# Key and query scalings split by token slot in five blocks, with a new issue order

## The chip, the core and the metric

The kernel runs on one core of one Trainium2 chip. Its five engines work from queues of their own, each in order: TensorE (PE) for matrix products, VectorE (DVE), ScalarE (ACT) and GpSimd (POOL) for elementwise work, SyncE (SP) for starting transfers. ACT can start transfers too. The metric is the device time of one execution in microseconds (us). Three runs of the kernel before took 165.88, 166.98 and 167.26 us; the median is 166.98 us.

## What is computed

Two layers follow each other. The first is a gated linear attention, a recurrence over 768 tokens for each of 4 batches and 8 heads of 48 channels; the second is a mixer that first mixes tokens and then channels.

```
for t in range(S):                       # q, k, v, alpha: (4, 8, 768, 48)
    state = alpha[:, :, t, :, None] * state + k_t (outer) v_t
    y[:, :, t] = q_t @ state
x = y as (4, 768, 384)
h  = relu(x^T @ w_tok1) @ w_tok2         # over tokens, 768 -> 256 -> 768
u  = x + h^T
h2 = relu(u @ w_ch1) @ w_ch2             # over channels, 384 -> 1536 -> 384
out = u + h2
```

Inputs and output are float32.

## The kernel before, in words

The recurrence is worked out in blocks. A block is 256 tokens of one batch with all its heads, so there are 12 blocks, numbered n = 0 to 11, three to a batch. A partition holds a pair of neighbouring tokens; the two places in the pair are called slot 0 and slot 1, so an input tile is 128 partitions x 8 heads x 2 slots x 48 channels. Within a block the decay is made from logarithms: `ln` takes the logarithm of alpha, `cum` (on PE, with a triangular matrix) sums it up along the tokens, and `E` and `IE` are the exponentials of the sums and of their negatives. Queries are multiplied by E and keys by IE; then an ordinary masked product of the two gives the part of the attention that lies inside the block, and a state carried from half block to half block gives the rest.

The names of a block's operations, with the block's number behind them:

- `ld_at`, `ld_kt`, `ld_qt`, `ld_vt`: loads of alpha, k, q and v (384 KB each, L534)
- `ln`, `cumw`, `E`, `Et`, `IE` for blocks 0 to 2, where each slot has sums of its own (WIDE); for blocks 3 to 11 `P` (product of the two alphas of a pair, L578), `ln1`, `lnP`, `r1`, `cum`, `E`, `IE`, with one sum per pair. There slot 0 of the keys is first multiplied by alpha of slot 1 (`k0a`, L634), and slot 0 of the queries by an inverse (`q0r`, L638)
- `kk` and `qq` (L642): the scalings of all 768 columns (2 slots x 8 heads x 48) of keys by IE and of queries by E, to bf16. They run on DVE or POOL
- `trk`, `trq` (L655): transposes of scaled keys and queries on PE; `evk`, `evq`: their eviction from PSUM. Blocks 6 to 11 have DMA transposes in their place (`dk`, `dq`) and `pq`
- `G0_`, `G1_` and `mask0_`, `mask1_`: the inner products and their masking (L709, DVE); `vb`, `vs0_`, `vs1_`: v cast to bf16, and its halves exchanged; `ka`, `kb`, `kc`: halves of the scaled keys moved between partitions for the state's product `K`; `s`, `sa`, `sm`: the state; `ia`, `ib`, `y0_`, `y1_`: products into the output; `x0_`, `x1_`: its eviction to a tile x of 128 tokens

The six x of a batch feed its mixer: `t1` (L791), `ht` (relu), `t2` (L796), `u` (sum with x), `up` and `ut` (transposes on PE and their eviction, for batches 0 and 1; DMA transposes `ux` for 2 and 3), `c1` (L815), `rt` (relu, L786 on ACT, L788 on DVE), `c2` (L820), `o` (L824) and `st` (store, L574). A `c1` or `c2` group is three matmuls of 384 columns. The weights come in 16 loads (`ldw_`) and are cast to bf16 by DVE, ACT or POOL (`cw_`).

Nothing decides the order of the work at run time. The table ORDER lists every operation with its engine (t PE, s ACT, v DVE, g POOL, y SP), and each engine gets its operations in the order of that list; the table BUFS gives each tile its buffer. Both were written out by a planner, which worked with the costs that stand in the code beside each operation. `f1_` and `f3_` are one or three fillers: products of zeros on PE whose result nobody uses. Operations marked `port=True` on DVE and POOL are made to follow each other where the list goes from one of the two engines to the other: `shared` (L673) adds a wait for the last such operation of the other engine. Dependences between tiles, and the reuse of a buffer, become semaphore waits. In the kernel before, SP starts all 48 input loads, all weight loads and 22 of the 25 stores, and ACT the other three.

Of the kernel before, what the change touches and what calls it, by code (L numbers as in the profile page):

```python
# [11 lines left out]
ALU = mybir.AluOpType  # L12
# [82 lines left out]
B, H, S, D = 4, 8, 768, 48  # L95
HD, DT, DCH = 384, 256, 1536
NB = 3
NX = 6
KFN = 3
# [16 lines left out]
def build(g):  # L116
# [12 lines left out]
    def attention(n):  # L129
# [5 lines left out]
        def O(name, eng, i, **kw):  # L135
            return P.op(f"{name}{n}", eng, pr(i), **kw)
# [20 lines left out]
        else:  # L157
# [16 lines left out]
        kk = O("kk", either(dve(768), pool_tt(768)), 5, writes=[pkk], reads=[kt, IE], port=True, preds=k_in + [e2],  # L174
               emit=lambda e: g.scaled(e, pkk, kt, IE, wide))
        qq = O("qq", either(dve(768), pool_tt(768)), 5, writes=[pkq], reads=[qt, E], port=True, preds=q_in + [e1],
               emit=lambda e: g.scaled(e, pkq, qt, E, wide))
# [3 lines left out]
        if n < NX:  # L181
            bk, bq = V("one"), V("one")
            trk = O("trk", pe([128] * 8), 8, writes=[bk], reads=[pkk], preds=[kk] + fill("trk", bk),
# [3 lines left out]
            trq = O("trq", pe([128] * 8), 8, writes=[bq], reads=[pkq], preds=[qq] + fill("trq", bq),  # L187
# [3 lines left out]
        else:  # L191
            evk = O("dk", {"SP": (1240.0, 1240.0)}, 9, writes=[tpk], reads=[pkk], preds=[kk],
                    emit=lambda e: g.xbar(tpk, pkk), dma=("x", 1400.0, 1180.0, 480.0))
            tqx = V("tpk")
            xq = O("dq", {"SP": (1240.0, 1240.0)}, 9, writes=[tqx], reads=[pkq], preds=[qq],
# [19 lines left out]
        if turned:  # L215
            vs = [vsw(hf, [vc]) for hf in range(2)]
            kx, kp_in = None, [kk, vc, vs[0]]
            if nst == 2:
                kx = V("kt")
                ka = shift("ka", 9, [kx], [pkk], [kk], lambda e: g.kturn(e, kx, pkk, 0))  # L220
                kb = shift("kb", 9, [kx], [pkk], [kk], lambda e: g.kturn(e, kx, pkk, 1))
                kp_in += [ka, kb, vs[1]]
            kc = shift("kc", 9, [pkk], [], [kk, trk if n < NX else evk] + ([ka] if nst == 2 else []),
# [4 lines left out]
        else:  # L228
            KO = O("K", {"PE": (344.0 if nst == 2 else 172.0, 420.0)}, 9.5, writes=[kp], reads=[pkk, vb],
                   preds=[kk, vc] + fill("K", kp) + ([prev_s[1]] if prev_s and k > 0 and n > NB else []),  # L230
# [146 lines left out]
ut_0_0v G0_3t G1_3t mask1_3v cw_wc11s ldw_wc22y up_0_2t ib3t ka4g q0r4g qq4g c1_0_0_0t c1_0_2_0t ld_at6y y1_3t
c1_0_1_0t ut_0_2s rt_0_0_0v x1_3v mask0_3v rt_0_1_0s ldw_wc24y ldw_wc23y sm1_3g trk4t cw_wc12s c1_0_2_1t c1_0_3_1t
c1_0_0_1t c1_0_1_1t c1_0_4_1t rt_0_2_0v rt_0_3_1s rt_0_1_1v trq4t cw_wc13s rt_0_0_1s rt_0_2_1s cw_wc14g cw_wc15g
rt_0_4_1v c1_0_6_0t c1_0_7_1t ldw_wc25y evq4v c1_0_9_1t y0_3t rt_0_9_1v P5v evk4s rt_0_6_0s x0_3v c1_0_8_1t c1_0_7_0t  # L380
rt_0_7_1s kc4s c1_0_10_1t c1_0_11_1t vb4g kb4g lnP5s rt_0_7_0s k0a5g ln15s ld_vt5y rt_0_10_1v cum5t G1_4t mask1_4v
rt_0_11_1s r15s rt_0_8_1s G0_4t c1_0_4_0t c1_0_3_0t IE5s mask0_4v vs0_4g ld_at7y kk5v c1_0_10_0t c1_0_5_0t c1_0_5_1t
rt_0_4_0s cw_wc20s c1_0_8_0t q0r5v c1_0_9_0t c1_0_6_1t rt_0_3_0s E5s rt_0_8_0s rt_0_5_1s c1_0_11_0t rt_0_5_0s
rt_0_6_1s trk5t qq5v vs1_4v ia4t y0_4t cw_wc21g rt_0_11_0s K4t trq5t evk5v sa0_4v c2_0_1_0t rt_0_9_0s sm0_4v
rt_0_10_0v cw_wc24g sa1_4v P6v ld_at8y sm1_4v kc5v vb5g cw_wc22s c2_0_5_0t c2_0_2_0t evq5s x0_4s cw_wc23s cw_wc25s
lnP6s ld_kt6y c2_0_2_1t c2_0_5_1t t1_1_1_0t G1_5t G0_5t P7g vs1_5g t1_1_1_1t c2_0_1_1t c2_0_1_2t c2_0_5_2t ld_qt6y
c2_0_1_3t c2_0_5_3t vs0_5s mask0_5v ld_at9y ld_vt6y c2_0_2_2t mask1_5v cum6t o_0_1v o_0_5v K5t c2_0_2_3t ia5t y0_5t
ib4t sa0_5v ln16s sm0_5v o_0_2v lnP7s k0a6g y1_4t cum7t t1_1_1_2t t1_1_0_0t x1_4v ib5t E6s y1_5t t1_1_0_1t t1_1_0_2t
x0_5s c2_0_3_0t r16s ln18s t1_1_0_3t x1_5v t1_1_0_4t t1_1_1_3t t1_1_0_5t IE6s t1_1_1_4t q0r6v kk6v t1_1_1_5t c2_0_0_0t
st_0_5y ld_kt7y ht_1_0s ht_1_1s ld_qt7y st_0_1y c2_0_3_1t t2_1_5t vb6s t2_1_0t E7s u_1_5v t2_1_2t t2_1_3t t2_1_4t  # L390
t2_1_1t u_1_2v u_1_3v c2_0_0_1t c2_0_3_2t qq6g ln17s k0a7g c2_0_0_2t u_1_0v c2_0_4_0t up_1_1t u_1_4v c2_0_3_3t u_1_1v
up_1_0t IE7s P8g ut_1_1v dk6y up_1_2t ka6g kb6s ut_1_0s r17s vs0_6s c2_0_4_1t c2_0_0_3t ld_at10y ld_vt7y o_0_3v
ut_1_2v dq6y kk7g dk7y c1_1_10_1t c1_1_9_1t c1_1_1_1t rt_1_10_1v r18s rt_1_1_1s vs1_6g kc6g lnP8s c1_1_2_0t ld_qt8y
P10v o_0_0v K6t vb7s q0r7g c2_0_4_2t cum8t s0_6v sa1_6v P9g c1_1_2_1t c1_1_0_1t c1_1_10_0t c1_1_3_0t qq7g vs1_7g kb7s
ld_vt8y E8s lnP10s rt_1_0_1s rt_1_2_1v rt_1_10_0v ld_kt8y c1_1_4_1t ld_qt9y rt_1_2_0v rt_1_9_1v ka7s vs0_7s sm1_6v
c2_0_4_3t c1_1_7_0t ld_kt9y dq7y c1_1_11_0t ld_vt9y st_0_0y lnP9s IE8s c1_1_8_1t rt_1_4_1s o_0_4v kc7s rt_1_7_0s
c1_1_9_0t cum9t c1_1_11_1t c1_1_1_0t c1_1_0_0t rt_1_8_1s rt_1_11_1s rt_1_1_0s pq6s ln19s q0r8v rt_1_3_0v rt_1_11_0v
rt_1_9_0v c1_1_5_0t qq8g K7t c1_1_5_1t k0a8g rt_1_0_0v rt_1_5_0v c1_1_3_1t rt_1_3_1s rt_1_5_1s c1_1_6_1t c1_1_7_1t
sa0_7v c1_1_4_0t sm0_7v r19s rt_1_7_1s ld_kt10y dq8y sa1_7v c1_1_6_0t rt_1_6_1v IE9s G0_6t G1_6t rt_1_6_0s rt_1_4_0s
kk8g E9s vb8s ln110s vs1_8s pq7s q0r9g ld_qt10y mask0_6v c2_1_4_0t k0a9g c2_1_4_1t dk8y c2_1_1_0t mask1_6v kk9g ib6t  # L400
# [478 lines left out]
```

## Time and profile before

| what | value |
|---|---|
| median of three runs | 166.98 us |
| profiled run, its own time | 167.16 us |
| span of the profiled run | 165.5 us |
| PE busy | 153.9 us, 93% |
| DVE busy | 113.5 us, 69% |
| ACT busy | 98.7 us, 60% |
| POOL busy | 77.4 us, 47% |
| read from HBM | 25.17 MB |
| granted PE clock | 1.0 in every slice |

The span runs from the first to the last instruction of one profiled execution; the run's time has a little around it. Busy times are sums over an engine's instructions. In the views below, an instruction's row gives its start, its duration, its engine and line, the tiles written and read, and in brackets how long the engine stood idle before it and what ended that. Rows that group instructions give their count, the busy time, the mean duration in ns and the idle time before them. The chain that ended last goes back from the last instruction to what released each step.

### The profile page before, as it was taken

How to read it: one execution, taken by the hardware profiler on the slowest of the kernel's cores; microseconds unless marked ns; L12 is line 12 of the kernel's file. 1: busy time of each engine (PE TensorE's matmuls, PEld its weight loads, DVE VectorE, ACT ScalarE, POOL GpSimd, SP SyncE). 2: the span in 40 equal slices, each digit the busy share in tenths (PEclk: the TensorE clock that was granted, in tenths of full speed). 3: DMA queues.
4: the chain of work that ended last, by engine and by line, in shares of the span. 5: the costliest groups of instructions: out<-in, count | busy, mean ns of one | idle time of the engine just before them, and what ended most of it. 6: DMA issues, size and time to landing. Idle time of an engine off the chain costs nothing.

```text
span 165.5 us, 4049 instructions
## 1 busy us (share of the span) xinstructions
PE 153.9 (93%) x1599; PEld 97.9 (59%) x1599; DVE 113.5 (69%) x200; ACT 98.7 (60%) x186; POOL 77.4 (47%) x87
## 2 busy tenths in 40 slices
PE   7849799799999999999999999999899999999992
PEld 2425657376667576665666676665566656566660
DVE  4059999698989987667776888985686703544232
ACT  3776699897999765589899965526502304162100
POOL 4055575899643344876689698397320000000000
PEclk9999999999999999999999999999999999999999
DMA  4999999999999799999999999889401362030114
GB/s 126 318 280 307 275 307 347 350 330 303 263 354 366 199 279 284 270 230 280 218 281 168 263 240 155 189 176 238 120 0 51 111 127 95 19 128 0 48 55 182
DMA packets 76322, 34.46 MB, mean 208 GB/s; under 512 B 68112, under 2 KB 76304, under 8 KB 76304
## 3 DMA queue, kind: packets, MB, share of 16 engines
q1 hardware_dynamic: 75872, 33.63, 78.9%
q10 hardware_dynamic: 432, 0.59, 1.0%
q8 instruction: 12, 0.20, 0.5%
q14 instruction: 6, 0.05, 0.1%
HBM read 25.17 MB, written 4.72 MB: 181 GB/s over the span
## 4 chain that ended last, share of the span: by engine, by line
PE 64%; DMA 13%; POOL 6%; SPq 4%; ACT 4%; issue 3%; DVE 2%; POOLq 0%; DVEq 0%
PE ps L820 26%; PE ps L815 20%; PE ps L593 9%; DMA in<-in_v_dram 6%; DMA in<-in_q_dram 5%; PE ps L791 4%; POOL pkq L642 3%; PE ps L796 3%; SPq L534 3%; DMA tpk<-pkq 3%; PE ps L655 1%; POOL in L638 1%; DVE pkk L642 1%; ACT vb L686 1%; PE ps L807 1%
## 5 line engine op out<-in xcount | busy, mean ns | idle before, releaser
L820 PE MATMUL ps<-wc,rt 128*128 128x384 bf16 (+2 forms) x300 | 53.2, 320 | 0.0
L815 PE MATMUL ps<-ut,wc 128*128 128x384 bf16 x288 | 50.9, 326 | 0.1
L786 ACT ACTIVATE rt<-ps 128x384 bf16<-128x384 f32 x59 | 26.9, 493 | 28.0 <-PE ps L815 27.7
L815 PEld LDWEIGHTS <-wc 128*128 128x128 bf16 x288 | 27.4, 98 | 17.7 <-issue 0.4
L820 PEld LDWEIGHTS <-rt 128*128 128x128 bf16 x300 | 27.6, 98 | 16.7
L709 DVE TENSOR_TENSOR gtm<-ps,mk 128x1024 bf16<-128x1024 f32 x24 | 28.5, 1219 | 4.6 <-PE ps L593 3.4
L788 DVE TENSOR_SCALAR rt<-ps 128x384 bf16<-128x384 f32 x37 | 19.4, 553 | 13.3 <-PE ps L815 13.2
L824 DVE TENSOR_TENSOR o<-ps,u 128x384 f32<-128x384 f32 (+2 forms) x25 | 13.1, 536 | 12.9 <-PE ps L820 12.9
L642 POOL TENSOR_TENSOR pkq<-in,E 128x768 bf16<-128x768 f32 x9 | 16.3, 1816 | 5.2 <-DVE in L638 3.3
L642 POOL TENSOR_TENSOR pkk<-in,IE 128x768 bf16<-128x768 f32 x7 | 12.7, 1817 | 9.4 <-ACT E L626 7.5
L686 ACT CAST vb<-in 64x384 bf16<-64x384 f32 (+1 forms) x22 | 14.1, 640 | 3.6 <-DMA in<-in_v_dram 2.3
L800 DVE TENSOR_TENSOR u<-ps,x 128x384 bf16<-128x384 f32 x24 | 12.1, 552 | 3.9 <-PE ps L796 3.6
L593 PE MATMUL ps<-zs 128*128 128x512 bf16 x30 | 9.7, 457 | 2.6 <-ACT IE L626 1.2
L791 PE MATMUL ps<-x,wt 128*128 128x384 bf16 x48 | 11.1, 326 | 0.0
L796 PE MATMUL ps<-ht,wt 128*128 128x384 bf16 x48 | 9.9, 327 | 0.8 <-POOL wt L687 0.8
L634 POOL TENSOR_TENSOR in<-in,in 128x384 f32<-128x384 f32 x8 | 8.0, 999 | 5.7 <-DVE pkk L687 2.6
L686 ACT CAST x<-ps 128x384 bf16<-128x384 f32 x12 | 5.5, 480 | 7.9 <-PE ps L593 7.8
L754 DVE TENSOR_TENSOR tmp<-ps,ss 128x384 f32<-128x384 f32 x16 | 8.8, 553 | 0.7 <-PE ps L593 0.3
L687 POOL CAST vb<-in 64x384 bf16<-64x384 f32 (+1 forms) x12 | 7.0, 581 | 4.8 <-DMA in<-in_v_dram 2.4
L593 PE MATMUL ps<-tpq,tpk 48*64 48x128 bf16 (+1 forms) x288 | 8.2, 219 | 0.8 <-POOL tpq L687 0.7
L757 POOL TENSOR_TENSOR ss<-tmp,E 128x384 bf16<-128x384 f32 x9 | 7.5, 834 | 3.0 <-PE ps L593 1.6
L593 PE MATMUL ps<-vb,gtm 128*128 128x48 bf16 x192 | 8.7, 184 | 0.0
(91 smaller groups left out, 208.2 us busy)
## 6 DMA issues: line engine op xcount, KB each, us to landing
in<-in_alpha_dram SPq DMA_DIRECT2D x12, 384.0 KB, 5.4
in<-in_q_dram SPq DMA_DIRECT2D x12, 384.0 KB, 5.6
in<-in_k_dram SPq DMA_DIRECT2D x12, 384.0 KB, 5.6
in<-in_v_dram SPq DMA_DIRECT2D x12, 384.0 KB, 5.5
in<-in_moe_w_ch_dram SPq DMA_DIRECT2D x12, 384.0 KB, 6.3
out_dram<-o SPq DMA_DIRECT2D x20, 192.0 KB, 2.4
in<-in_moe_w_tok_dram SPq DMA_DIRECT2D x4, 384.0 KB, 5.5
out_dram<-o ACTq DMA_DIRECT2D x3, 192.0 KB, 1.9
```

What stands on the lines that cost most here:

```text
L593: return self.pe.matmul(out, lhsT=lhsT, rhs=rhs, start=start, stop=stop, skip_group_check=True)
L642: self.shared(self.eng[e].tensor_tensor(self.t(dst)[:, :, :, 0:D], self.t(src).rearrange("p h s d -> p s h d"), bass.AP(tensor=f.tensor, o ...
L686: return self.act.copy(d, s)
L709: self.nc.vector.tensor_tensor(self.t(gtm)[:, hf, :, :], self.pair(gp).rearrange("p a (j t) -> p (a j) t", t=128), bass.AP(tensor=m.tensor ...
L786: self.act.activation(d, s, AF.Relu)
L788: self.nc.vector.tensor_scalar_max(d, s, 0.0)
L791: self.pe.matmul(self.bank(bank)[:, 0:HD], lhsT=self.wt1[:, kc, m * 128 : m * 128 + 128], rhs=self.t(x), start=(kc == 0), stop=(kc == NS - 1))
L796: self.pe.matmul(self.bank(bank)[:, 0:HD], lhsT=self.wt2[:, kc, i * 128 : i * 128 + 128], rhs=self.t(hts[kc]), start=(kc == 0), stop=(kc = ...
L800: self.nc.vector.tensor_tensor(self.t(u)[:, i % 3], self.bank(bank)[:, 0:HD], self.t(x), ALU.add)
L815: self.pe.matmul(self.bank(bank)[:, 0:HD], lhsT=self.wc1[:, kc, mc * 128 : mc * 128 + 128], rhs=self.t(ut)[:, 3 * half : 3 * half + 3, kc, ...
L820: self.pe.matmul(self.bank(bank)[:, 0 : cz - ca], lhsT=self.t(rts[mc][0])[:, i * 128 : i * 128 + 128], rhs=self.wc2[:, mc, ca:cz], start=( ...
L824: self.nc.vector.tensor_tensor(self.t(o)[:, ca:cz], self.bank(bank)[:, 0 : cz - ca], self.t(u)[:, i % 3, ca:cz], ALU.add)
```

## The change

Blocks 0 to 4 (SPLIT) scale keys and queries in two instructions of 384 columns each, one per slot. `kk` and `qq` are then the half of slot 1, which in blocks 3 and 4 depends on the load only; `kl` and `ql` are the half of slot 0, which waits for `k0a` or `q0r`. Whoever read the whole result now waits for both halves. The tables ORDER and BUFS are new throughout.

```
+SPLIT = (0, 1, 2, 3, 4)
...
-        kk = O("kk", either(dve(768), pool_tt(768)), 5, writes=[pkk], reads=[kt, IE], port=True, preds=k_in + [e2],
-               emit=lambda e: g.scaled(e, pkk, kt, IE, wide))
-        qq = O("qq", either(dve(768), pool_tt(768)), 5, writes=[pkq], reads=[qt, E], port=True, preds=q_in + [e1],
-               emit=lambda e: g.scaled(e, pkq, qt, E, wide))
+        slots = ((1,), (0,)) if n in SPLIT else ((0, 1),)
+
+        def scale(names, dst, src, f, pre, raw):
+            return [O(nm, either(dve(384 * len(sl)), pool_tt(384 * len(sl))), 5, writes=[dst], reads=[src, f], port=True,
+                      preds=(pre if 0 in sl else raw) + ([e2] if f is IE else [e1]),
+                      emit=lambda e, sl=sl: g.scaled(e, dst, src, f, wide, sl)) for nm, sl in zip(names, slots)]
+
+        kk = scale(("kk", "kl"), pkk, kt, IE, k_in, [ld["kt"]])
+        qq = scale(("qq", "ql"), pkq, qt, E, q_in, [ld["qt"]])
...
-    def scaled(self, e, dst, src, f, wide):
-        f = self.t(f)
+    def scaled(self, e, dst, src, f, wide, slots):
+        f, c, z = self.t(f), slots[0], len(slots)
         self.shared(self.eng[e].tensor_tensor(
-            self.t(dst)[:, :, :, 0:D], self.t(src).rearrange("p h s d -> p s h d"),
-            bass.AP(tensor=f.tensor, offset=f.offset, ap=[list(f.ap[0]), [HD if wide else 0, 2], [D, H], [1, D]]),
-            ALU.mult))
+            self.t(dst)[:, c : c + z, :, 0:D], self.t(src)[:, :, c : c + z, :].rearrange("p h s d -> p s h d"),
+            bass.AP(tensor=f.tensor, offset=f.offset + (c * HD if wide else 0),
+                    ap=[list(f.ap[0]), [HD if wide else 0, z], [D, H], [1, D]]), ALU.mult))
```

What the new tables change, in the parts that the prediction speaks of:

| | before | after |
|---|---|---|
| fillers (single products of zeros) | 30 | 33, of which 7 (before 13) ahead of the first sums |
| input loads issued by SP / ACT | 48 / 0 | 29 / 19 |
| stores issued by SP / ACT | 22 / 3 | 13 / 12 |
| weight casts on ACT / POOL / DVE | 10 / 6 / 0 | 7 / 8 / 1 |
| `ht` on ACT / DVE | 5 / 3 | 7 / 1 |
| first loads in order | at0 at1 at3 qt0 kt0 vt0 vt1 kt1 at2 | at0 kt0 at1 vt0 qt0, at3 (ACT), kt1 at2 |

ACT's list up to the two relus of the first token product, after the change (`ld_` are the loads that it issues):

```
ln0 ln1 E0 ld_at3 IE0 IE1 Et1 vb0 E1 Et0 ld_qt2 evq0 ln13 ln2 vb1 ld_kt3 lnP3 vs0_0 IE2 Et2 E2 ld_vt2 IE3 vs1_1 E3 evq1
x1_0 evq2 x0_0 vb2 vs0_1 cw_wt10 r13 x0_1 vs1_2 lnP4 kb3 vb3 ka3 x0_2 vs1_3 ld_qt4 kc3 ht_0_1 ht_0_0
```

and before:

```
ln0 ln1 E0 Et0 ln13 IE0 IE1 E1 vb0 r13 vb1 vs0_0 lnP3 Et1 ln2 Et2 E2 IE2 evq1 x0_0 x1_0 E3 IE3 lnP4 vb2 evq2 cw_wt10
cw_wt11 x0_1 x1_1 vs1_2 vb3 vs1_3 vs0_3 kc3 ht_0_1
```

POOL's list from block 3 on, after: `q0r3 ql3 cw_wc10 cw_wc11 k0a4 kk4 kl4 q0r4 qq4 ql4 cw_wc14`; before: `q0r3 cw_wt20 qq3 k0a4 cw_wc10 kk4 ka4 q0r4 qq4`. The halves stand on DVE for block 0 (all four), block 2 (all four) and qq3, and on POOL for block 1, kk3, kl3, ql3 and block 4. The last piece of the output, in columns 0 to 319 and 320 to 383, was finished with the wide part last and is now finished with the narrow part last.

150 lines of the change are left out of this document (75 added, 75 removed), and 22 rows, old and new, of the table BUFS.

## The prediction

> **What bounds the kernel now.** I read the page's first part, then the busy time by stage, then the chain that ended last, and then each engine's instructions in order of time up to the first channel matmul.
>
> ```profile
> span 165.5 us, 4049 instructions
> ...
> PE 153.9 (93%) x1599; PEld 97.9 (59%) x1599; DVE 113.5 (69%) x200; ACT 98.7 (60%) x186; POOL 77.4 (47%) x87
> ```
>
> The span is 165.5 us of a run that took 167.16 us, so 1.66 us lie outside it. TensorE is busy for 153.9 us of it.
>
> ```profile
> 25.00:30.00 5.00, 4.87 (x87) 3.54 (x83) 5.00 (x7) 4.59 (x9) 2.57 (x5) 1.00 1.12 347
> 30.00:35.00 5.00, 3.71 (x37) 2.31 (x38) 3.50 (x8) 4.19 (x8) 5.00 (x5) 1.00 1.11 339
> ...
> 110.00:120.00 10.00, 9.42 (x61) 5.64 (x60) 6.33 (x14) 5.70 (x13) 6.32 (x8) 1.00 0.73 172
> ```
>
> ```profile
> 36.50:70.00 33.50, 33.50 (x342) 22.44 (x339) 28.70 (x46) 25.89 (x52) 18.97 (x22) 1.00 1.02 292
> ```
>
> ```profile
> 70.00:94.70 24.70, 24.26 (x262) 15.20 (x260) 18.40 (x33) 23.13 (x44) 18.67 (x16) 1.00 1.17 243
> ```
>
> In these rows the first pair after the length is PE, the third DVE, the fourth ACT, the fifth POOL. From 36.5 to 70 us PE never stops; between 70 and 94.7 us it loses 24.70 - 24.26 = 0.44 us, and between 110 and 120 us 0.58 us. So after 36.5 us about 1.0 us (these two) is all that a better order could win back on PE. Before that PE idles or runs fillers, and the time is set by how soon the first channel matmul, c1_0_0_0, can start.
>
> ```profile
> 31.64 1.62 PE L796 MATMUL ps<-ht,wt 128*128 128x384 bf16 x8 [0.85 <-POOL wt L687]
> ...
> 33.42 0.62 PE L655 MATMUL ps<-idn,pkq 128*128 128x128 bf16 x8 [0.16 <-POOL pkq L642]
> ...
> 36.52 1.14 PE L815 MATMUL ps<-ut,wc 128*128 128x384 bf16 x6
> ...
> 41.07 0.61 PE L655 MATMUL ps<-idn,pkq 128*128 128x128 bf16 x8
> ```
>
> ```profile
> 21.99 7.64 DMA in<-in_q_dram
> ...
> 29.77 0.99 POOL in L638
> 30.76 0.82 POOL wt L687
> ...
> 162.22 0.49 DVE o L824
> ```
>
> The first fence is PE's own order, the second the chain that ended last. c1_0_0_0 starts at 36.52 us. The second token product (L796) waited 0.85 us for a weight cast on POOL, which stood behind q0r3, which waited for the load of qt3; trq3 at 33.42 us waited 0.16 us for the query scaling on POOL. I count the PE work ahead of c1_0_0_0 in both orders: it is the same set of operations, fillers aside. Hence the sum: time after = time before + shift of c1_0_0_0 + change of PE's waits behind it + change of the tail behind PE's end at 162.22 us.
>
> **The change, part by part.** *The two halves.* The rows of the groups by shape:
>
> ```profile
> L642 POOL TENSOR_TENSOR pkq<-in,E 128x768 bf16<-128x768 f32 x9 | 16.3, 1816 | 5.2 <-DVE in L638 3.3 <-DVE pkk L642 1.7
> ...
> L638 POOL TENSOR_TENSOR in<-in,lf 128x384 f32<-128x384 f32 x5 | 5.0, 996 | 2.2 <-DMA in<-in_q_dram 1.4 <-ACT la L584 0.7
> ...
> L642 DVE TENSOR_TENSOR pkk<-in,IE 128x768 bf16<-128x768 f32 x5 | 4.8, 953 | 0.0
> ...
> L638 DVE TENSOR_TENSOR in<-in,lf 128x384 f32<-128x384 f32 x4 | 2.2, 554 | 0.0
> ```
>
> A scaling of 384 columns is not in the trace; the nearest rows are L638's products of that size. Two of them are 2 x 996 - 1816 = 176 ns dearer on POOL and 2 x 554 - 953 = 155 ns on DVE. Of the ten scalings of blocks 0 to 4, five have both halves on POOL (kk1, qq1, kk3, kk4, qq4), four on DVE (block 0 and block 2), and that of block 3's queries is shared. That adds 0.9 us to POOL and 0.6 us to DVE, at least nothing and at most this, since queued instructions overlap a little. What it can win is an early start of the raw half, and the order uses it little: in blocks 0 to 2 neither half needs another product first, and in block 4 both halves are queued behind k0a4 and q0r4 or next to them. Only qq3 (DVE) goes ahead of its other half, by which trq3 comes free of the 0.16 us wait. DVE's extra is hidden by ACT, as the next part shows; without that cover it is 0.6 us. POOL's pair in block 4 is not hidden, see below.
>
> *Loads on ACT's queue.* This is the larger part: 19 of the 48 input loads and 12 stores are now issued by ACT, where before 3 stores were. What an issue costs:
>
> ```profile
> 0.81 0.46 SPq L534
> ...
> 1.33 0.56 SPq L534
> ...
> 1.94 1.26 SPq L534
> ```
>
> ```profile
> L534 SPq DMA_DIRECT2D in<-in_q_dram x12: 433/1150/1507, 3.2 to 106.2; - x12
> ```
>
> ```profile
> L574 ACTq DMA_DIRECT2D out_dram<-o x3: 338/377/444, 156.6 to 161.0; - x3
> ```
>
> SP's first two loads took 0.46 and 0.56 us, all others while the queue was full 1.15 us in the median; ACT's three stores, late and alone, 0.377 us. ACT has one load under way at a time, so I take 0.45 us, near the first row, and keep 0.38 and 1.15 us as the ends. The Trainium skill, page "DMA: Bandwidth & Descriptors", section "Issuing engines are not separate DMA queues", says that transfers started from several engines run on the same DMA engines and interleave, and that only the issuing sequencer's time is saved. The trace agrees as far as it goes: the DMA share in the rows above is already 1.12 and 1.11 at 25 to 35 us with one queue. By that rule nothing is gained in transfer time; without it the 19 loads could shorten the stream, so it lowers the chance of my faster case.
>
> ```profile
> 4.44 0.84 ACT L587 ACTIVATE la<-in 128x768 bf16<-128x768 f32 x1 [2.35 <-DMA in<-in_alpha_dram]
> 5.62 0.84 ACT L587 ACTIVATE la<-in 128x768 bf16<-128x768 f32 x1 [0.34 <-DMA in<-in_alpha_dram]
> ...
> 31.88 0.83 ACT L686 CAST wt<-in 128x768 bf16<-128x768 f32 x1 [0.56 <-DMA in<-in_moe_w_tok_dram]
> ```
>
> ```profile
> 8.95 0.96 DVE L642 TENSOR_TENSOR pkq<-in,E 128x768 bf16<-128x768 f32 x1 [5.61 <-DMA in<-in_q_dram]
> ```
>
> These are landings seen by those who waited: the first load 4.44 us, the second 5.62, the fourth 8.95, the 21st (wt2's second piece) 31.88: (31.88 - 4.44) / 20 = 1.37 us a load. The loads ahead of that piece are the same 20 in both orders, so it still lands near 31.9 us. One wait is new: SP's issue of wt1's second piece takes the buffer of qt1 and so waits for qq1 on POOL, near 19 us (10.3 us for qt0 as worked out below, four halves on DVE, seven shorter products and copies on POOL); vt3, qt3 and both pieces of wt2 stand behind it on SP. By then 15 loads are issued, and at 1.37 us each they last to 4.44 + 14 x 1.37 = 23.6 us, which covers the stop. But at1 is now third: 5.62 + (8.95 - 5.62) / 2 = 7.3 us, so ACT's ln1 starts 1.6 us later.
>
> *ACT up to the relus of the token hidden (ht).* Pitches, start to start:
>
> ```profile
> 22.24 0.52 ACT L584 ACTIVATE la<-in 128x384 bf16<-128x384 f32 x1
> 22.67 0.81 ACT L686 CAST vb<-in 128x768 bf16<-128x768 f32 x1
> 23.39 1.31 ACT L686 COPY tpq<-ps 128x1024 bf16<-128x1024 bf16 x1
> 24.61 0.83 ACT L686 CAST wt<-in 128x768 bf16<-128x768 f32 x1
> ...
> 30.25 0.49 ACT L786 ACTIVATE ht<-ps 128x384 bf16<-128x384 f32 x1
> ```
>
> 384 columns take 0.43 us, 768 take 0.72, 1024 take 1.22. Before, ACT issues from ln1 to ht_0_1 14 of 768, 2 of 1024, 16 of 384 and 3 tiny ones (0.1): 10.1 + 2.4 + 6.9 + 0.3 = 19.7 us, from 5.62 us; ht's start at 30.25 us shows about 5 us of waits in it. After, from ln1 to the second ht: 13 of 768, 3 of 1024 (evq0 comes from DVE), 20 of 384 (both ht, vs1_1, vs0_1, ka3, kb3 and x0_2 come, vs0_3 and x1_1 go), 3 tiny, and 5 loads: 9.4 + 3.7 + 8.6 + 0.3 + 2.25 = 24.2 us. From 7.3 us that ends at 31.5 us without any wait. Going down the queue I find about 0.9 us that stay: vb2 behind vt2's load, which ACT itself issues only after E2, and little else, as more queued work swallows waits. So both ht are done at 32.4 us (ends: 31.5, and 34 with half of before's waits), and the token product starts there instead of at 31.64 us.
>
> DVE's x copies come before that. In the row
>
> ```profile
> 28.05 1.08 DVE L687 CAST x<-ps 128x384 bf16<-128x384 f32 x2
> ```
>
> the last two x of batch 0 ended at 29.1 us. qt0 is now the fifth load, 8.95 + 1.37 = 10.3 us, so DVE starts 1.4 us later; evq0 (1.2), kk1 and kk3 (0.95 each) leave it, block 0's key halves and k0a3 (0.55 each) and three splittings (0.16 each) come, a net of -1.0 us. So DVE ends its x near 29.5 us, and ACT its own last one, x0_2, five entries ahead of the end, at 32.4 - 4 x 0.43 - 0.45 = 30.2 us: 0.7 us of cover for DVE. Behind ht, ACT casts wt2's second piece, makes E4, IE4 and ln14, evicts trq3 and then copies ut_0_1: 32.4 + 0.72 + 0.43 x 3 + 1.22 + 0.43 (r14) + 0.72 = 36.8 us, where c1_0_0_0 starts: **+0.2 us** (36.52 before). The wait on POOL goes, since the wt2 cast is now DVE's, and ACT is late in its place. Ends: -1.3 us (wt2's piece at 31.9 + cast 0.7 + product 0.3 + sum 0.5 + transposes 0.5 + copy 0.7, and some issue gaps, makes 35.2 us) and +3.3 us (1.15 us an issue).
>
> *trq4.* On POOL now stand cw_wc10, cw_wc11, k0a4, kk4, kl4, q0r4, qq4, ql4. kt4's load went behind both weights and is the 24th: 4.44 + 23 x 1.37 = 35.9 us. Six products of 996 ns end at 42.0 us. PE reaches trq4 after ten channel groups of three matmuls (0.49 us each) and two small y: 36.8 + 4.9 + 0.4 = 42.1 us; before, it was there at 41.07 us. A tie; with the qt4 load of ACT pushing in between I take **+0.3 us** (0 to 1). Nothing else waits there but PE's order behind it.
>
> *Second mixer's channel stage.* From the first c1_1 to the first t1_2 ACT had 39 x 0.43 + 3 x 0.72 + 3 x 1.22 = 22.6 us to do beside PE's 24.7 us (the row 70.00:94.70 covers almost all of it). After, it has 43, 2 and 3 and six loads: 18.5 + 1.4 + 3.7 + 2.7 = 26.3 us, beside PE's stage that grew by four c2 groups to about 26.6 us. An engine that full, in order, with waits, will hold PE's banks now and then: before lost 0.44 us at 92%, I take 1.2 us at 99%: **+0.8 us** (0 to 4).
>
> *Tail.*
>
> ```profile
> out_dram<-o SPq DMA_DIRECT2D x1, 160.0 KB, 1.8
> ...
> out_dram<-o SPq DMA_DIRECT2D x1, 32.0 KB, 1.5
> ```
>
> The last eviction was of 320 columns (0.49 us) and its store 1.8 us; now the 64-column piece is last, and the large one overlaps twelve narrow matmuls: **-0.4 us** (0 to -0.5).
>
> Sum: 0.2 + 0.3 + 0.8 - 0.4 = +0.9 us, so 168.1 us against 167.16 us of the profiled run; the median of 166.98 us is 0.18 us lower, so I predict **167.9 us**. About 1% (1.7 us) is what measuring this kernel can tell from no change.
>
> **The rivals.** *ACT late in both places* (0.20): waits persist as before, ht ends at 34 us, +1.5 us at c1_0_0_0, and the c1_1 stage gives 26.3 us plus half of 2 us of waits, +1.8 us; trq4 is then free; -0.4: 170 us. For it: ACT's busy 23.13 of 24.70 us. Against: waits shrink as queues fill.
>
> *An ACT issue costs 1.15 us* (0.10): +3.3 us at c1_0_0_0, 6 x 0.7 = 4.2 us more in the c1_1 stage, most of it on PE: about 174 us. It decides from some 0.6 us an issue. Against: the rows of ACT's stores.
>
> *Faster* (0.20): ACT's queue has the slack that I deny it, c1_0_0_0 starts 1.3 us earlier, SP, freed of loads, ends half of the 1.0 us of waits, and the tail gives 0.4: -2.2 us, 164.8 us. For it: both waits of the token product on POOL are gone. Against: 24.2 us of queue from 7.3 us on.
>
> *A cold PE* (0.06):
>
> ```profile
> 4.02 0.15 PEld L593 LDWEIGHTS <-zs 128*128 128x128 bf16 x1 [0.28 <-issue]
> 4.45 0.15 PEld L593 LDWEIGHTS <-zs 128*128 128x128 bf16 x1 [0.28 <-issue]
> ```
>
> ```profile
> 8.88 1.02 PE L593 MATMUL ps<-zs 128*128 128x512 bf16 x4 [1.21 <-ACT IE L626]
> ```
>
> The first fillers follow each other by 0.43 us, later ones by about 0.25. Only 7 instead of 13 now stand ahead of the first sums, and then nothing until ln0 ends at 5.3 us. If PE stays at the slow pace until 16 us, trq0, K0, trk0 and trk1 (0.6 us each) double, DVE ends 2.4 us later and, past its cover and ACT's three entries ahead of ht, c1_0_0_0 0.9 us: 168.8 us. The Trainium skill, page "TensorE: Matmul & The Clock Gate", section "What's actually happening", puts the faster clock after about 3.4 us of sustained activity; by that rule this happens, and 7 x 0.43 = 3.0 us of fillers are a little short of it.
>
> That the halves do nothing is no rival in time: I already give them almost none.
>
> **How the numbers follow.** My case has 0.44, with its own range 166.7 to 169.2 us. Faster by over 1% (below 165.3) is nearly all of the faster case, 0.18; slower by over 1% (above 168.65) is ACT's two cases, half of the cold one and the upper end of mine, 0.40; the rest 0.42. The range 164.8 to 170.5 leaves out the dear issue and the edges.
>
> **What would show it.** ACT's two ht end near 32.4 us and c1_0_0_0 starts near 36.8 us; ACT issues of 0.4 to 0.5 us; trq4 near 42.1 us with a wait for POOL of under 1 us; halves of about 1.0 and 0.55 us; PE's waits behind 36 us near 2.1 us, most where c1_1 runs, named after ACT. PE waits of several us after 100 us, which I did not work out, or a load stream off its 1.37 us would make it wrong.

## The result, and the profile after

The changed kernel takes 167.90 us in the median (166.40 to 169.47) where the kernel before, measured beside it, takes 166.64 us: a ratio of 1.0072, with a 95% interval of 1.0044 to 1.0100. It is a little slower, by less than the 1% named above. Ratios and intervals leave out executions more than 1.5% above the fastest of the same kernel and medians keep them, which matters below for e5 alone: its four longest, 169.10 to 170.36 us, are not in its ratio. The profiled execution of the changed kernel took 168.94 us, one of its longer ones, at a mean PE clock of 0.98; its start of the channel stage is therefore set further down beside that of e6, the changed kernel with 14 fillers more, at clock 1.00.

The first parts of the page of the changed kernel:

```profile
span 167.2 us, 4054 instructions
## 1 busy us (share of the span) xinstructions
PE 156.6 (94%) x1602; PEld 99.8 (60%) x1602; DVE 112.6 (67%) x203; ACT 99.3 (59%) x191; POOL 74.4 (45%) x89
...
PEclk9969998799999999999999999999999999999999
```

The span is 1.7 us longer, and PE's clock, full in every slice before, is 6 to 8 tenths in three slices of the first fifth. PE's own order, with the rows that answer to those quoted of before:

```profile
25.82 0.50 PE L599 MATMUL ps<-vb,pkk 64*128 64x96 bf16 x8 [1.75 <-ACT vb L692]
...
37.93 4.06 PE L821 MATMUL ps<-ut,wc 128*128 128x384 bf16 x24
...
43.21 0.61 PE L661 MATMUL ps<-idn,pkq 128*128 128x128 bf16 x8
```

The state product of block 2, K2, waits 1.75 us for ACT's cast of v. The first channel matmul, c1_0_0_0, starts at 37.93 us, 1.41 us later than before (36.52); the transposes trq4 wait for nothing. The stretches behind it:

```profile
5.00:10.00 5.00, 3.36 (x29) 1.78 (x29) 0.74 (x2) 3.07 (x5) 0.00 (x0) 0.76 1.17 324
10.00:15.00 5.00, 4.57 (x64) 3.14 (x63) 3.36 (x7) 4.49 (x9) 3.49 (x5) 0.90 1.17 325
15.00:20.00 5.00, 5.00 (x68) 3.10 (x66) 4.50 (x8) 4.56 (x10) 2.71 (x3) 1.00 1.15 335
20.00:25.00 5.00, 3.93 (x52) 2.49 (x52) 4.71 (x7) 2.92 (x5) 3.02 (x4) 1.00 1.15 337
25.00:30.00 5.00, 4.06 (x60) 3.02 (x60) 3.10 (x4) 4.87 (x9) 2.77 (x4) 0.80 1.01 322
...
70.00:95.00 25.00, 24.78 (x256) 15.49 (x254) 20.10 (x36) 22.59 (x45) 15.83 (x16) 1.00 1.05 224
```

In the stage of the second mixer PE loses 25.00 - 24.78 = 0.22 us, not the 1.2 us forecast. The clock (the number behind POOL's pair) is 0.76 and 0.90 up to 15 us and 0.80 from 25 to 30 us; in slices of 1 us it is 0.50 to 0.52 from 28 to 31 us, some 2 us behind the end of K2's wait. So the loss lies ahead of c1_0_0_0. ACT's own order there, with the loads that it issues as ACTq:

```profile
14.58 0.83 ACT L692 CAST vb<-in 128x768 bf16<-128x768 f32 x1 [0.52 <-DMA in<-in_v_dram]
14.66 0.37 ACTq L540 DMA_DIRECT2D in<-in_k_dram  x1
...
16.68 0.37 ACTq L540 DMA_DIRECT2D in<-in_v_dram  x1
...
24.94 1.37 ACT L692 CAST vb<-in 128x768 bf16<-128x768 f32 x2 [2.08 <-DMA in<-in_v_dram]
...
32.53 0.87 ACT L792 ACTIVATE ht<-ps 128x384 bf16<-128x384 f32 x2 [0.28 <-PE ps L797]
```

ACT issues vt2, the values of block 2, at 16.68 us and waits for them until 24.94 us; before, vb2 started at 22.67 us without a wait. In the chain that ended last this load is the longest transfer ahead of c1_0_0_0:

```profile
16.68 8.24 DMA in<-in_v_dram
```

Why so late? In the list vt2 is the 14th load and stands ahead of wt1's first piece and of at4. But SP does not wait for ACT:

```profile
12.92 2.28 SPq L556 DMA_DIRECT2D in<-in_moe_w_tok_dram  x1
15.30 0.45 SPq L540 DMA_DIRECT2D in<-in_alpha_dram  x1
18.48 0.37 SPq L556 DMA_DIRECT2D in<-in_moe_w_tok_dram  x1
```

SP had issued wt1's first piece and at4 before 16.68 us, so vt2 was the 16th load to be issued. From the first landing, 4.35 us, the forecast's 1.37 us a load gives 4.35 + 15 x 1.37 = 24.9 us for the 16th load and 22.2 us, before ACT asked for it, for the 14th.

That the first figure is what ACT saw is partly chance. By the trace the first twelve loads landed 1.21 us apart, the twelfth at 17.6 us. vt2 landed as the 17th, behind wt1's second piece, which was issued 1.8 us later and landed at 24.6 us. ACT's queue moved 0.02 MB from 22 us on, so all but a twentieth of vt2's 384 KB was there by 22 us. The landing thus depends on what else is under way and not on the count alone; why the last packets came so late, no run shows.

My theory for the experiments: vt2 is issued too late behind other loads, and what hangs on it (vb2, K2, the last x of batch 0, ht) is the loss. The rival is the forecast's own, ACT's longer queue with its issues; a third is PE's lower clock, a fourth the halves.

### The profile page after: what moved, and what is told of

It is laid out like the page before. It is cut to its first block, busy times and chain, and to the rows that moved or that the text cites. A ratio compares the mean times of both kernels' runs of the same rounds, so it can differ in the third digit from the quotient of the medians.

```text
span 167.2 us, 4054 instructions
## 1 busy us (share of the span) xinstructions
PE 156.6 (94%) x1602; PEld 99.8 (60%) x1602; DVE 112.6 (67%) x203; ACT 99.3 (59%) x191; POOL 74.4 (45%) x89
## 4 chain that ended last, share of the span: by engine, by line
PE 57%; DMA 13%; issue 7%; ACT 6%; POOL 6%; DVE 4%; SPq 2%; POOLq 1%; DVEq 0%; ACTq 0%
PE ps L826 22%; PE ps L821 18%; PE ps L599 9%; DMA in<-in_q_dram 6%; DMA in<-in_v_dram 5%; PE ps L797 4%; DMA tpk<-pkq 3%; PE ps L802 2%; ACT rt L792 2%; SPq L540 2%; POOL in L584 2%; PE ps L661 1%; POOL in L644 1%; POOL pkq L648 1%; POOL ss L763 1%
## 5 line engine op out<-in xcount | busy, mean ns | idle before, releaser
L826 PE MATMUL ps<-wc,rt 128*128 128x384 bf16 (+2 forms) x300 | 54.7, 319 | 0.3 <-ACT rt L792 0.3
L794 DVE TENSOR_SCALAR rt<-ps 128x384 bf16<-128x384 f32 x39 | 20.5, 551 | 12.3 <-PE ps L821 12.2
L648 POOL TENSOR_TENSOR pkk<-in,IE 128x384 bf16<-128x384 f32 (+1 forms) x10 | 13.2, 1325 | 13.7 <-DVE pkk L648 8.6
L648 POOL TENSOR_TENSOR pkq<-in,E 128x384 bf16<-128x384 f32 (+1 forms) x9 | 12.2, 1362 | 6.1 <-ACT rt L792 2.4
L797 PE MATMUL ps<-x,wt 128*128 128x384 bf16 x48 | 12.4, 334 | 0.0
L599 PE MATMUL ps<-zs 128*128 128x512 bf16 x33 | 10.9, 454 | 1.1 <-DVE zs L502 1.1
L693 POOL CAST vb<-in 64x384 bf16<-64x384 f32 (+1 forms) x14 | 8.6, 615 | 7.0 <-DVE ss L763 2.6
L648 DVE TENSOR_TENSOR pkq<-in,E 128x384 bf16<-128x384 f32 (+1 forms) x8 | 5.5, 701 | 6.0 <-DMA in<-in_q_dram 5.9
L644 POOL TENSOR_TENSOR in<-in,lf 128x384 f32<-128x384 f32 x7 | 7.0, 998 | 5.6 <-DVE ss L763 3.2
L599 PEld LDWEIGHTS <-gtm 128*128 128x128 bf16 x192 | 8.0, 100 | 1.9 <-issue 0.2
```

The costliest lines, as they stand in the source:

```text
L599: return self.pe.matmul(out, lhsT=lhsT, rhs=rhs, start=start, stop=stop, skip_group_check=True)
L648: self.shared(self.eng[e].tensor_tensor(self.t(dst)[:, c : c + z, :, 0:D], self.t(src)[:, :, c : c + z, :].rearrange("p h s d -> p s h d") ...
L794: self.nc.vector.tensor_scalar_max(d, s, 0.0)
L797: self.pe.matmul(self.bank(bank)[:, 0:HD], lhsT=self.wt1[:, kc, m * 128 : m * 128 + 128], rhs=self.t(x), start=(kc == 0), stop=(kc == NS - 1))
L826: self.pe.matmul(self.bank(bank)[:, 0 : cz - ca], lhsT=self.t(rts[mc][0])[:, i * 128 : i * 128 + 128], rhs=self.wc2[:, mc, ca:cz], start=( ...
```

## The experiments

All rows in one table: start of c1_0_0_0, the span behind it, the median and the ratio to the kernel before. The medians of the kernel before that stand beside the other rows' ratios were 166.5 to 166.7 us.

| kernel | c1_0_0_0, us | span behind it, us | median, us | ratio, 95% interval |
|---|---|---|---|---|
| before | 36.52 | 129.0 | 166.64 | 1 |
| after | 37.93 | 129.3 | 167.90 | 1.0072 [1.0044, 1.0100] |
| e1: after, vt2 early, by SP | 35.95 | 128.5 | 166.17 | 0.9971 [0.9940, 1.0001] |
| e2: after, all loads by SP | 37.26 | 128.8 | 168.17 | 1.0079 [1.0046, 1.0112] |
| e12: after, vt2 early, by ACT | 36.57 | 128.5 | 166.85 | 1.0018 [0.9986, 1.0050] |
| e10: e1, the 15 later ACT loads by SP | 35.63 | 129.9 | 167.39 | 1.0068 [1.0033, 1.0103] |
| e6: after, 14 fillers | 37.57 | 128.3 | 167.68 | 1.0060 [1.0031, 1.0088] |
| e7: e1, 9 fillers at the head | 35.78 | 128.9 | 166.82 | 1.0009 [0.9976, 1.0041] |
| e8: e1, halves merged | 36.18 | 128.3 | 166.34 | 0.9994 [0.9966, 1.0022] |
| e9: before, halves split | 35.02 | 129.8 | 166.50 | 0.9993 [0.9963, 1.0023] |
| e5: before, vt2 late | 35.87 | 128.9 | 168.42 | 1.0036 [0.9992, 1.0080] |
| e11: e5, 9 fillers | 36.75 | 129.3 | 167.31 | 1.0027 [0.9997, 1.0058] |
| e13: e1, ln14, r14, sa1_3 behind ut | 36.26 | 128.4 | 166.56 | 0.9994 [0.9964, 1.0024] |
| e14: e1, ln14, r14 behind ut | 35.66 | 128.2 | 165.81 | 0.9973 [0.9940, 1.0007] |

**The load of block 2's values.** e1 takes the one entry from ACT's queue and puts it where SP reaches it early:

```
- ... E2s qq2v ql2v ld_vt2s ib0t cum3t ldw_wt10y ...
+ ... evk1v ld_kt2y ld_vt2y G0_0t ...
```

> The changed kernel with one load moved: block 2's v is issued by SP directly behind block 2's keys instead of by ACT behind E2, so it stands ahead of the first weight piece and block 4's alpha in the stream of loads. Load-order theory (the time is lost because vt2 lands at 24.9 us and holds vb2, K2 and the rest of batch 0): vb2 starts at 23 us or before with no wait for a load, c1_0_0_0 near 36.6 us instead of 37.9, the run 1.0 to 1.4 us under the changed kernel, ratio to the kernel before about 1.000. Rival (ACT's queue is too long because it issues loads): one issue of 0.4 us less, c1_0_0_0 at most 0.4 us earlier, ratio about 1.005. Rival (the halves cost it): no difference, 1.007.

ACT and PE of e1:

```profile
22.71 0.47 ACT L692 CAST x<-ps 128x384 bf16<-128x384 f32 x1
23.20 1.37 ACT L692 CAST vb<-in 128x768 bf16<-128x768 f32 x2
...
30.55 0.87 ACT L792 ACTIVATE ht<-ps 128x384 bf16<-128x384 f32 x2
```

```profile
24.34 0.51 PE L599 MATMUL ps<-vb,pkk 64*128 64x96 bf16 x8
...
35.95 1.30 PE L821 MATMUL ps<-ut,wc 128*128 128x384 bf16 x7
```

Both waits are gone, the two relus start at 30.55 us instead of 32.53 and c1_0_0_0 at 35.95 us instead of 37.93. The median is 1.73 us lower, and the interval lies wholly below that of the changed kernel. One entry of the order carries the whole loss. It moved two things at once, though, the time of the issue and the queue, and two further runs take them apart.

e12 leaves the load to ACT and moves it up in ACT's order, by nine entries (not four, as its expectation counts):

```
- ... E2s qq2v ql2v ld_vt2s ib0t ...
+ ... mask0_0v G1_0t P3g ld_vt2s ln13s ql1g ...
```

> The changed kernel with one entry of its order moved: block 2's values are still loaded by ACT, but four instructions of ACT's order earlier, ahead of ln13 (near 12.8 us instead of 16.7). With this the two questions stand apart: place in the stream (here early) and issuing queue (here ACT). If the place alone decides: ACT's wait for that load shrinks from 2.08 us to under 0.5, the two relus of the token hidden start near 31 us instead of 32.5, c1_0_0_0 near 36 to 36.5 us, and the time goes to 0.997 to 1.001 of the kernel before. If ACT's queue is what costs: the time stays at 1.005 to 1.008 and c1_0_0_0 near 37.5.

ACT issued it at 11.55 us, and its wait for it went. The ratio came to 1.0018, just above the place's forecast and under the queue's 1.005, though the interval's end touches that. The price is a new one. POOL's queries of block 1 in e12, and then in e1:

```profile
17.25 1.96 POOL L648 TENSOR_TENSOR pkq<-in,E 128x384 bf16<-128x384 f32 x2 [1.42 <-DMA in<-in_q_dram]
```

```profile
16.79 1.96 POOL L648 TENSOR_TENSOR pkq<-in,E 128x384 bf16<-128x384 f32 x2 [0.70 <-DMA in<-in_q_dram]
```

The wait for block 1's queries doubled, and PE's transposes trq1 waited 0.39 us behind it: c1_0_0_0 at 36.57 us, between the two others. The trace has the landings: v came at 18.3 us in e12 and at 21.1 us in e1, but block 1's queries at 17.2 instead of 16.7 us and block 2's keys at 20.4 instead of 18.0 us. The load that is moved forward holds up those under way beside it.

e2 keeps the list as it is and lets SP issue all 19 loads:

```
- ld_at3s ... ld_qt2s ... ld_kt3s ... ld_vt2s ... ld_qt4s ...
+ ld_at3y ... ld_qt2y ... ld_kt3y ... ld_vt2y ... ld_qt4y ...
```

> The changed kernel with all 19 loads of ACT issued by SP, at the same places of the list. ACT-issue theory of the prediction (0.45 us of ACT an issue): ACT's queue up to ht is 2.2 us shorter, ht ends 1 us or more earlier and the second mixer's stage loses its waits, ratio about 0.998. Load-order theory: ACT gains nothing by it, since its issues ran beside its other instructions; vt2 now goes ahead of the first weight piece, but at3 and qt2 go ahead of at2 and vt1, which land 2 loads (2.6 us) later, so the time moves by less than 0.6 us either way from the changed kernel.

With no load on ACT's queue the time is what it was, 1.0079. So taking the issues off ACT does not remove the loss. The place of the loss changed: in one queue the list's order holds, at3 and qt2 go ahead of kt1, and PE's trk1 waits 0.94 us for POOL, while vb2 waits for nothing. e2 does not weigh ACT's issues by themselves, since it moves the later loads too, which has a price of its own, as the next run shows; that the issues cost ACT nothing rests on ACT's rows and on e12.

e10 is e1 with only the first three of ACT's 18 loads left there and the 15 later ones by SP:

```
- ld_qt4s ... ld_vt4s ... ld_kt5s ...
+ ld_qt4y ... ld_vt4y ... ld_kt5y ...
```

> The changed kernel with block 2's v loaded early, and the 15 later loads that ACT issues (from block 4's queries on) issued by SP at the same places of the list; at3, qt2 and kt3 stay with ACT. If an ACT issue takes ACT's time (0.45 us each, as the prediction had it): the stage of the second mixer's channel products loses ACT load, PE's waits of 0.2 to 0.3 us there go, 0.3 to 0.8 us faster, ratio 0.993 to 0.995. If it runs beside ACT's other work: no gain, and SP's in-order waits can only delay loads: 0.997 to 1.003.

c1_0_0_0 stays early, 35.63 us, but the span behind it is 1.4 us longer than in e1. The stretch in which it is lost:

```profile
95.00:120.00 25.00, 23.72 (x283) 15.03 (x275) 19.65 (x33) 11.16 (x24) 16.66 (x17) 1.00 0.91 178
```

PE stands 1.28 us there, 0.68 of it behind POOL's `pq`, where e1 loses 0.30 and the changed kernel 0.26 in the same stretch. SP runs its DMA transposes there in between; that these and the loads hold each other up is likely, but not tested apart. So for the later loads ACT's queue is worth about 1% with this list.

**The halves.** e8 merges them in e1 at the place of the later half (SPLIT empty), e9 splits them in the kernel before:

```
-SPLIT = (0, 1, 2, 3, 4)
+SPLIT = ()
```

> The same early load, with the ten scalings of blocks 0 to 4 in one instruction of 768 columns again, each where the later of its two halves stood and on its engine (block 3's queries on DVE). If the halves are worth nothing, as forecast: same time within 0.3 us (0.997), since the extra 0.16 to 0.18 us a scaling is covered. If they are what the new order lives on: slower by 0.5 us or more. If they cost: faster by 0.3 us or more.

> The kernel before with nothing but the split: each of the ten scalings of blocks 0 to 4 in two halves, one behind the other, in its old place and on its old engine; order and buffers as before. My theory: the price of the halves by itself, 0.155 us on DVE and 0.176 us on POOL for each scaling, on the path only at qq3 and qq4 and partly at kk2 and qq2: +0.2 to +0.5 us, ratio 1.001 to 1.003. Rival (the halves are the loss): 1.007.

Neither can be told from no change: e9 is at 0.9993, and e8's interval overlaps that of e1. In e9's profile c1_0_0_0 starts 1.5 us earlier than in that of before, and 0.8 us of it come back behind it. Much of the 1.5 us is a difference between executions: block 0's queries, the fourth load in both and issued at nearly the same time (3.14 and 3.24 us), held DVE up until 8.95 us in the profile of before, but in e9's only until here:

```profile
8.06 1.03 DVE L648 TENSOR_TENSOR pkq<-in,E 128x384 bf16<-128x384 f32 x2 [4.74 <-DMA in<-in_q_dram]
```

e11, further down, has 7.94 us for the same wait. So the one profile of before is an execution whose loads came some 0.9 us late, and places that are set beside its 36.52 us are uncertain by as much. The prices, by shape in the changed kernel:

```profile
L648 POOL TENSOR_TENSOR pkq<-in,E 128x768 bf16<-128x768 f32 x4 | 7.3, 1817 | 3.7 <-ACT rt L792 2.4 <-DVE kt L693 1.2
...
L648 POOL TENSOR_TENSOR pkq<-in,E 128x384 bf16<-128x384 f32 x5 | 4.9, 999 | 2.4 <-DVE pkq L648 1.6 <-DMA in<-in_q_dram 0.7
```

**The clock.** e6 adds 14 products of zeros to the changed kernel: six at the head, three between the first two sums, five ahead of K2.

```
+ f3_trk0t f3_trq0t ... f3_cumw1t ... f1_G02t f3_K2t f1_K2t
```

> The changed kernel with 14 more fillers on PE, nothing else: 6 at the head, 3 between the first two sums, 5 ahead of K2, where PE stood idle. Clock theory (PE's lower granted clock, 0.76 to 0.90 at 5 to 15 us and 0.80 to 0.85 at 25 to 35 us, costs part of the loss): granted clock 1.0 from 5 us on in every run, ratio about 1.003. Load-order theory: the clock rises as well, but ht still waits for block 2, so the gain is at most the 0.3 us of slower matmuls behind 26 us: ratio about 1.005.

Its clock is 1.00 throughout and its times are narrow, 167.40 to 168.43, but their middle is where it was. ACT's wait for the load stays:

```profile
24.82 1.37 ACT L693 CAST vb<-in 128x768 bf16<-128x768 f32 x2 [1.50 <-DMA in<-in_v_dram]
```

So the late load is still there when the clock is cured. How much of the 1.0072 is the clock's is open all the same. Of the changed kernel's own 16 executions the four at a clock of 0.999 or more took 166.40 to 167.57 us, the six at 0.98 or less 167.70 to 169.47 us; e6, at full clock, is not as fast as the four, so its fillers may cost something of their own. e7 adds the first nine of these fillers to e1, in the same places:

```
+ f3_trk0t f3_trq0t ... f3_cumw1t
```

> The changed kernel with block 2's v loaded early (as in the run before) and 9 more fillers at the head, 6 ahead of the first sums and 3 between the first two. Clock theory: PE's granted clock, 0.74 at 5 to 10 us there, is 1.0, the first sums and transposes are up to 0.5 us faster each, and the first chain gains: ratio about 0.995. Load-order theory: the early chain waits for loads (qt0, vt1, vt2), so only the clock changes: ratio 0.997 as without fillers, within 0.1%.

Nothing is won: 1.0009, above the 0.997 expected, though the intervals overlap. Within e1, too, the clock (0.74 from 5 to 10 us in its profile) shows no price: its eight executions at a mean clock of 0.99 or less took 165.42 to 166.71 us, the four at 0.998 or more 165.57 to 166.79 us.

e5 does the reverse in the kernel before: vt2 goes behind kt3 and wt1's first piece.

```
- Et1s ld_vt2y K1t ... ldw_wt10y qq1g
+ Et1s K1t ... ldw_wt10y ld_vt2y qq1g
```

> The kernel before with one load moved: block 2's v goes behind block 3's keys and the first weight piece, two places later in SP's order. Load-order theory: vt2 lands 2 x 1.3 = 2.6 us later, near 24.5 us, ACT waits for it at vb2 (22.67 us before), K2 and all of block 2 follow 1.5 to 1.9 us later, c1_0_0_0 1.0 to 1.5 us later, ratio 1.006 to 1.009. Rivals (halves, ACT's issues): no difference, 1.000.

Its times fall in two groups, 166.28 to 166.92 us at a clock of 0.997 or more, and 168.39 to 170.36 us, all but one of these at 0.98 or 0.99. The profile, one of the lower group, does not show the later start that was expected: c1_0_0_0 is at 35.87 us, ahead of the 36.52 us of before. e11 adds nine fillers (the 13 of its expectation is a miscount) near block 1's and 2's transposes and K2:

```
+ f1_trq1t f3_trq1t ... f3_trq2t ... f1_K2t f1_G02t
```

> The kernel before with block 2's values loaded late (behind kt3 and wt1's first piece), as in the run whose times fell in two groups, and 13 more products of zeros where PE waits between 14 and 26 us. If the clock gate makes the two groups (a gap on PE just long enough to lower the clock in some executions): the times close up to 166.3 to 167.2 us, clock 1.00, ratio 0.998 to 1.002. If the late load itself costs, through landings that differ from execution to execution: still two groups or a spread of over 2 us, or a median near 168 us.

The upper group is gone: 166.46 to 168.04 us, every clock at 0.997 or more. So the upper group goes with the clock, but for the one at 1.00. The middle stayed higher than expected of that alone, by the late load or by the fillers themselves. ACT's row in e11, and in the profile of e5:

```profile
24.46 0.83 ACT L686 CAST vb<-in 128x768 bf16<-128x768 f32 x1 [2.58 <-DMA in<-in_v_dram]
```

```profile
23.55 0.83 ACT L686 CAST vb<-in 128x768 bf16<-128x768 f32 x1 [1.14 <-DMA in<-in_v_dram]
```

The wait is there in both, so the late load holds ACT up in that order too; what it costs there without the clock, 1.0027 with an interval that reaches 0.9997, can't be told from nothing.

**What is late next.** In e1 ACT has no gap from 20 to 36 us. e13 and e14 put work that nobody needs yet behind the copies ut, on which c1_0_0_0 depends; e13 moves sa1_3 on DVE as well.

```
- ... t2_0_4t ln14s t2_0_5t ... up_0_1t r14s G1_3t ... ut_0_1s ut_0_2s
+ ... t2_0_4t t2_0_5t ... up_0_1t G1_3t ... ut_0_1s ut_0_2s ln14s r14s
```

> The changed kernel with block 2's values loaded early from SP, as in the run that brought the load forward, and in addition three entries moved behind the copies that feed the first channel matmul: ln14 and r14 on ACT, sa1_3 on DVE. There ACT stands busy without a gap from 20 us to 36.8 us and DVE from 30.9 us, and c1_0_0_0 started at 35.95 us. If the start of c1_0_0_0 is bound by what is queued ahead of these copies: c1_0_0_0 near 35.3 to 35.6 us, ACT's copies 0.8 us earlier, and 0.992 to 0.996 of the kernel before. If PE's own work ahead of it, or POOL's scaling of block 4 that waits for r14, takes over: no change against that run (0.995 to 1.000), with a new PE wait at trq4 or at c1_0_0_0.

> The changed kernel with block 2's values loaded early from SP, and only ln14 and r14 of ACT behind the copies that feed the first channel matmul; DVE keeps its order. It repeats the early load, so it also says how firm that run's 0.997 is. If ACT's queue ahead of its two copies sets c1_0_0_0: 0.3 to 0.5 us earlier than that run's 35.95 us and 0.993 to 0.997 of the kernel before. If DVE's sums and its own copy, which end at the same time, set it: c1_0_0_0 at 35.7 to 36.1 us and 0.996 to 1.000.

In e13 sa1_3 reads its bank when a token product already stands in it, so the second half of block 3's state, and what follows from it, is not the reference's; instructions and sizes are e1's. Its PE row ahead of c1_0_0_0:

```profile
35.75 0.49 PE L813 MATMUL ps<-idn,u 128*128 128x128 bf16 x6 [0.65 <-DVE tmp L760]
36.26 4.11 PE L821 MATMUL ps<-ut,wc 128*128 128x384 bf16 x24
```

The third transposes wait 0.65 us for sa1_3's bank: PE's order takes over. e14, without that move, has c1_0_0_0 at 35.66 us:

```profile
35.11 0.51 PE L814 MATMUL ps<-idn,u 128*128 128x128 bf16 x6
35.66 4.06 PE L822 MATMUL ps<-ut,wc 128*128 128x384 bf16 x24
```

That is 0.29 us earlier than in e1. But the two relus of the token hidden, which stand ahead of the entries that were moved, start 0.29 us earlier too (30.55 us in e1):

```profile
30.26 0.87 ACT L793 ACTIVATE ht<-ps 128x384 bf16<-128x384 f32 x2
```

So moving ln14 and r14 won nothing. From the start of these relus to c1_0_0_0 it is 5.40 us in the profiles of the changed kernel, e1, e2, e6, e7, e10 and e14 alike, and in none of them does PE show a wait from the first product of ht on: PE's own work sets this stretch, and c1_0_0_0 moves with ht. Its ratio, 0.9973, repeats e1's: bringing the load forward gives 1% against the changed kernel and some 0.3% against the kernel before, at the limit of what these intervals show.

## Why the prediction was right, and where it was wrong

The time, 167.9 us, came out, and so did its direction; most of its terms did not, and that it came out to 0.1 us is luck.

- *The frame held.* The sum was the start of c1_0_0_0 plus what follows. In the table the start of c1_0_0_0 moves by 2.9 us and the span behind it by 1.7 us (128.2 to 129.9), so the second part is the steadier one but no constant.
- *ACT up to the relus of the token hidden (ht)*, +0.2 us at c1_0_0_0, was the step that failed. The mechanism was given as ACT's queue of 24.2 us with 0.9 us of waits. Measured, c1_0_0_0 moved by +1.41 us in the profile (+1.05 in e6, at full clock), against a start of before that is itself late by up to 0.9 us. From ln1 at 6.76 us to the end of both ht at 33.40 us, 1.0 us behind the forecast's 32.4, ACT's rows show 3.6 us of waits where the forecast had 0.9: 2.08 us for vt2, the load that I had named, and four of 0.28 to 0.52 us that were taken as swallowed. The rest, work and small gaps, was 23.0 us instead of 24.2 and began 0.5 us earlier than forecast, which hid part of it. The 0.9 us has no working in the forecast; by the list's place the load would have come before ACT asked for it. The path from the end of ht to c1_0_0_0 was not ACT's, as the forecast added it up, but PE's own work; at 4.5 us it is about as long as the 4.4 us forecast.
- *The stream of loads*, 1.37 us each, was too slow: wt2's second piece, the 21st load, was forecast near 31.9 us, its place in before, and landed at 29.0 us, 1.24 us a load. The pitch came from an execution whose fourth load was late (8.95 us). The *issue* of 0.45 us was 0.37 us for both loads shown, and it is not even a term: the rows at 14.58 and 14.66 us show an issue running beside ACT's instruction. The rival of 1.15 us is out by the same rows. The rule cited from the Trainium skill, page "DMA: Bandwidth & Descriptors", section "Issuing engines are not separate DMA queues", that a second issuing engine adds no transfer bandwidth, agrees as to the highest rate: from 5 to 15 us the engines move 324 to 325 GB/s in the changed kernel and in e2, where SP issues all. From 15 to 25 us it is 335 and 337 GB/s against 285 and 300 in e2, so the stream was steadier with two.
- *SP's stop behind qq1* was forecast near 19 us and ended at 18.48 us, and the cover claimed for it held: the DMA share is 1.17, 1.15 and 1.15 in the three stretches of 5 us from 10 to 25 us.
- *trq4, +0.3 us*: nothing, since c1_0_0_0 came late enough. *Second mixer, +0.8 us*: the other way, 0.22 us lost instead of 0.44. ACT was busy for 22.59 us in those 25 us, under the 26.3 us worked out, of which 2.7 were issues, so the fullness never came, and with it falls the rival of ACT late in both places. Behind c1_0_0_0 PE stands 1.55 us in all, not 2.1, and its longest wait, 0.8 us, is one for POOL between 120 and 130 us. *Tail, -0.4 us*: half of it, the span ends 3.1 us behind PE's last matmul instead of 3.3. Together +0.7 us were forecast behind c1_0_0_0; measured are +0.3 in the profile and -0.65 in e6, so with this order the stages behind are rather shorter, as far as single profiles tell. A start that was forecast too early and stages forecast too long made up for each other.
- *Halves*: on POOL 2 x 999 - 1817 = 181 ns dearer (176 forecast), and worth nothing that can be told either way (e8, e9).
- *Cold PE*: the premise came true in some executions: the clock from 5 to 10 us is 0.76 in the changed kernel's profile and 0.74 in e1's, but 1.00 in those of e2 and e12, with the same seven fillers. The rule cited from the Trainium skill, page "TensorE: Matmul & The Clock Gate", section "What's actually happening", that the faster clock comes after about 3.4 us of sustained activity, agrees with the first two and not with the other two. The price, 0.9 us, did not show: e7 wins nothing by curing it. The low clock that goes with long times was not named: the one behind K2's wait.
- *Faster* missed 164.8 us, but its direction was one entry away: e1, at the limit of what can be told from the kernel before.

## What to carry to other kernels

When loads are split over two issuing engines, order them by the time at which each engine reaches its issue, not by their place in a common list; then read from a trace when each one lands and hold that against the time at which the consumer asks. Place times a mean time per load is a first guess that was off by up to 2 us here (the 16th at 1.24 us a load would have come at 22.9 us, and vt2 came at 24.9). Split the span where the bound engine becomes busy for good, and judge what is ahead of that point and what is behind it separately: an order can win in one and lose in the other. One profile of each kernel is thin for this: two executions differed by 0.9 us in the landing of an early load. Where an engine's clock depends on its gaps, look at the spread of the times as well as at their middle.

## What the runs showed of the hardware

A load issued by ACT costs ACT's instructions nothing visible (0.37 us beside a cast of 0.83 us). Loads of two issuing queues need not land in the order of their issue: vt2, from ACT at 16.68 us, landed at 24.9 us, and a weight piece, from SP at 18.48 us, at 24.6 us. A gap on PE can have a price beyond itself, in some executions only: e5's two groups lie 2 us apart, and the upper one is gone with the fillers of e11; in the changed kernel the clock is 0.50 to 0.52 from 28 to 31 us, 2 us behind the end of a wait of 1.75 us, and full again from 32 us on. A low clock near the start, 0.74 from 5 to 10 us in e1, shows no such price.
